# Linear attention beside an MLP: the tiles of y and of the MLP's activations begin 16 bytes later

## The chip, the core and the metric

The kernel runs on one core of one Trainium2 chip. The metric is the device time of one execution in microseconds, as the median of several runs. The kernel before takes 721.05 us (three runs, 720.82 to 721.19).

## The reference

A token matrix x of 2048 rows and 640 columns is normalised twice over. One branch is attention in linear form with 32 heads of 20; the other is an MLP of width 1728. The result is x plus both.

```python
xn = layernorm(x)
# A: linear attention with a learned feature map
q, k, v = split(xn @ wqkv)                       # 32 heads of 20
pq, pk = q @ w_phi, k @ w_phi                    # per head
phi = concat([softmax(p), softmax(-p)])          # for pq and pk
kv, z = phi_k^T v, sum(phi_k)
o = (phi_q kv) / (phi_q z + 1e-6)
# B: MLP
y = layernorm(xn)
h = gelu(y @ w1 + b1)
out = x + o @ wo + (h @ w2 + b2)
```

## The kernel before

Tokens are the columns of most tiles: the 2048 tokens are four blocks of 512, and the 640 features are five chunks of 128 partitions (`KC = 5`). All matrix products are in float32r, and each float32 operand is split exactly into a high and a low part (`split`, line 57), so that one product is three matmuls: high by high, high by low, low by high (`mm3`, lines 69 to 72). TensorE therefore runs some 3,300 matmuls, nearly all with a stationary operand of 128x128 and a streamed one of 512 columns.

The stages, in order:

- The first tokens are normalised and turned on TensorE into y of block 0 (`make_y0`), and y of block 1 is made from the transposed x (`next_y`, lines 413 to 445): POOL subtracts the mean (L438), DVE multiplies (L440), ACT rounds to the high part (L442), DVE subtracts for the low part (L444).
- MLP on blocks 0 and 1 (`Mlp.passes`): w1 is stationary and y is streamed (L70 to L72, `bank<-y,w`), ACT applies gelu (L264), the result is split into the m tiles, and w2 is stationary with the m tiles streamed (L70 to L72, `bank<-m,w`). DVE adds into acc (L307, L309). Beside it run small matmuls that fold w_phi into the projection weights (L499), and y of blocks 2 and 3 is made and put into DRAM (L589).
- The projections, one token tile of 128 after the other, 16 in all (`proj`, L673): y is stationary here, 128 columns of it, and the folded weights wkh, wkl (512, 512 and 320 columns) and v's weights (512 columns) are streamed. For each tile ACT, POOL and DVE make the two softmax features of k and q (`features`, L697 to L711, then L719, L764, L770), and `kv_tile` (L743, L747) accumulates phi_k and v. y of blocks 2 and 3 is loaded at tile 4 and tile 8 (L789), for use four tiles later.
- MLP on blocks 2 and 3, with the attention's products beside it (L967 and L968: kvs is stationary, and the feature tiles ph and e are streamed).
- The output projection (L1128 to L1136, again `mm3`): wo is stationary and the attention's result is streamed. It is split into tiles of the y pool (`Attention.split`, L1028 to L1032).

The order on TensorE is written by hand for the whole kernel (`manual_schedule`), and that of DVE, ACT and POOL for parts of it; `mlp.beside` is a generator from which one step is drawn after each group of matmuls.

The tiles come from pools that lie one behind another in each partition. From the bottom: the scratch for descriptors of DMAs that POOL would issue (16,384 bytes), constants, acc0 and acc1, the pool `m` (six tiles m0 to m5, from `mtile`, line 117: gelu's output, the split activations, and in the projections the features), the pool `y` (four tiles y00, y10, y01, y11), `raw` and `w`. A second side grows down from the top: x, the folded weights wkh and wkl, later acc2, acc3, kvs, ph and the e tiles. In the program as built, y00 begins at byte 68,064 of a partition, m4 at 38,368, w0 at 114,144, wkh at 175,584, kvs at 203,232. Each of these is 32 more than a multiple of 64, and so are the other tiles and slices of these names that matmuls read: every chunk, half and head group lies a multiple of 64 bytes from its tile's start. The exceptions are the tiles that L743 streams, whose slices step by 240 bytes, and small operands of the transposes and of L499 and L901 to L913.

Of the kernel before, what the change touches and what calls it, by code (L numbers as in the profile page):

```python
# [9 lines left out]
F32R = mybir.dt.float32r  # L10
# [5 lines left out]
P = 128  # L16
S, D, F, H, DH = 2048, 640, 1728, 32, 20
KC = D // P
# [23 lines left out]
SPREAD = [0] * 20 + [1] * 10 + [2] * 2  # L42
EPS = 1e-5
DEN_EPS = 1e-6


def f(ap):
    return ap.bitcast(F32)
# [3 lines left out]
def tile_kernel(ctx: ExitStack, tc: tile.TileContext, x, xT, wkT, wqT, wv, wphi, wo, w1, b1, w2, b2,  # L52
                ident, mmask, emask, vsel, out):
    nc = tc.nc
    ctx.enter_context(nc.allow_low_precision(reason="float32 operands are split exactly into float32r parts"))

    def split(hi, lo, src, scale=None, eng=nc.vector, first=nc.scalar):

        if scale is None:
            if first is nc.scalar:  # L60
                nc.scalar.activation(hi, src, AF.Copy)  # L61
            else:
                first.tensor_copy(hi, src)
            eng.tensor_tensor(lo, src, f(hi), op=ALU.subtract)  # L64
        else:
            nc.scalar.activation(hi, src, AF.Copy, scale=scale)
            nc.vector.scalar_tensor_tensor(lo, src, scale, f(hi), op0=ALU.mult, op1=ALU.subtract)
# [43 lines left out]
    mp = ctx.enter_context(tc.tile_pool(name="m", bufs=1))  # L111
    ys = ctx.enter_context(ExitStack())
    yp = ys.enter_context(tc.tile_pool(name="y", bufs=1))
    rp = ys.enter_context(tc.tile_pool(name="raw", bufs=1))
    wp = ys.enter_context(tc.tile_pool(name="w", bufs=1))

    def mtile(i, dtype=F32):
        return mp.tile([P, 2, D if i < 5 else 512], dtype, name=f"m{i}")
    y = {}

    def load_x(ts, xp, tag="xb"):
# [89 lines left out]
    class Mlp:  # L211
# [55 lines left out]
        def passes(self, g, b, ws, hid=None):  # L267
# [5 lines left out]
            if hid is None:  # L273
                hid, todo, gts = [], ws, mtile(4)
# [58 lines left out]
    dmas[1][0]()  # L333
    nc.scalar.dma_start(b1t, b1)
    nc.scalar.dma_start(b2t, b2)
    y[0], y[1] = ([yp.tile([P, KC, 512], F32R, name=f"y{p}{b}") for p in range(2)] for b in range(2))
    gts = mtile(4)
    hid = [mtile(2 * j + 1, F32R) for j in range(2)]
    hid = [(h[:, 0, :512], h[:, 1, :512]) for h in hid]
# [322 lines left out]
    def proj(t, i):  # L662

        yh, yl = y[t // 4]
        c = slice((t % 4) * P, (t % 4) * P + P)
        wh, wl = [w[:, :, slice(*CB[i])] for w in wkv_] if i < 3 else wv_
        ps = ptile()[:, :wh.shape[2]]
        ops = [(lh, rh, kc) for kc in range(KC) for lh, rh in ((yh, wh), (yh, wl), (yl, wh))]
        if i == 3:

            ops.sort(key=lambda op: op[1] is wh)
        for n, (lh, rh, kc) in enumerate(ops):
            nc.tensor.matmul(ps, lh[:, kc, c], rh[:, kc], start=n == 0, stop=n == 3 * KC - 1)  # L673
        return ps
# [11 lines left out]
    def evacuate(ps, n, f0):  # L686

        p3 = pks[n].rearrange("p (h f) -> p h f", f=DH)
        src = ps.rearrange("p (f h) -> p h f", h=H)
        return nc.scalar.activation(p3[:, :, 1 + f0:1 + f0 + src.shape[2]], src, AF.Copy).ins  # L690
# [23 lines left out]
    def k_tile(t):  # L714
        e, sm = features(t, "k")
        w = kp.tile([P, 2 * H], F32, name="w")
        nc.vector.reciprocal(w, sm)
        e3 = e.rearrange("p s (h f) -> p (s h) f", f=DH)
        nc.gpsimd.tensor_tensor(e3, e3, w.unsqueeze(2).to_broadcast([P, 2 * H, DH]), op=ALU.mult)  # L719
        ft = wp.tile([P, 4, D], F32R, name="w1")  # L720
        fh, fl = ft[:, 0:2], ft[:, 2:4]
        split(fh, fl, e)
        return ft

    def v_parts(t, ps, d0):

        v = vbuf[t % 2].rearrange("p (g c) -> p g c", c=VS)
        rs = rs_all[:, t:t + 1]
        n = DH - d0 if d0 else VF
        parts = []  # L730
        for g, m, w in ((0, 11, 3 * n),) if d0 else ((0, 10, 3 * n), (10, 1, 2 * n)):
            src = ps[:, 3 * g * n:3 * g * n + m * w].rearrange("p (g c) -> p g c", g=m)
            parts.append((src, *(v[:, g:g + m, c + 3 * d0:c + 3 * d0 + w] for c in (3, 67))))
        for src, hi, lo in parts:
            last = nc.scalar.activation(hi, src, AF.Copy, scale=rs)
        for src, hi, lo in parts:
            nc.vector.scalar_tensor_tensor(lo, src, rs, f(hi), op0=ALU.mult, op1=ALU.subtract)
        return last.ins
# [15 lines left out]
    def q_tile(t):  # L754


        e, sm = features(t, "q")
        w = kp.tile([P, 2 * H], F32, name="w")
        nc.vector.reciprocal(w, sm)
        e = e.rearrange("p s f -> p (s f)")  # L760
        for (hs, sv), (_, wv_), (_, ev) in zip(by_head(sm, 1), by_head(w, 1), by_head(e, DH)):
            nc.gpsimd.tensor_tensor(wv_[:, 1], sv[:, 0], wv_[:, 1], op=ALU.mult)
            shape = list(ev[:, 1].shape)
            nc.gpsimd.tensor_tensor(ev[:, 1], ev[:, 1], wv_[:, 1].to_broadcast(shape), op=ALU.mult)  # L764

        b, i = divmod(t, 4)
        if i == 0:
            ets[b] = [places[n % 5] for n in range(4 * b, 4 * b + 4)]
        for n, et in enumerate(ets[b]):
            nc.vector.transpose(et[:, :, 32 * i:32 * i + 32], e[:, 320 * n:320 * n + 320].rearrange("p (j r) -> p j r", r=32))  # L770

    def store_phi(b, n):

        ed = e_dram[b][320 * n:320 * n + 320, :].rearrange("(j r) (q n) -> q r j n", r=32, q=4)
        for q in range(4):
            nc.sync.dma_start(ed[q], ets[b][n][32 * q:32 * q + 32])
# [7 lines left out]
    for t, i in [(t, i) for t in range(14) for i in range(4)] + TAIL:  # L784
        if (t, i) in ((4, 0), (8, 0)):
            b = t // 4 + 1
            y[b] = [yp.tile([P, KC, 512], F32R, name=f"y{p}{b % 2}") for p in range(2)]
            for p in range(2):
                nc.sync.dma_start(f(y[b][p]), y_dram[b - 2][p])  # L789
        ps = proj(t, i)  # L790
        pq = 1 + t % 3
        if t and t % 4 == 0:
            store_phi(t // 4 - 1, i)
        if i == 0:
            evac = evacuate(ps, 0, 0)
        elif i == 1:
            evac = evacuate(ps[:, :KQ - 512], 0, 512 // H)
            fts[t] = k_tile(t)
            evacuate(ps[:, KQ - 512:], pq, 0)
        elif i == 2:  # L800
            evacuate(ps[:, C3 - C2:], pq, B1F)
            v_parts(t, ps, VF)
            q_tile(t)
        else:
            evac = v_parts(t, ps, 0)

        tk = {(15, 1): 13, (15, 3): 14}[t, i] if (t, i) in ((15, 1), (15, 3)) else t - 2 if 1 < t < 15 and i == 0 else None
        if tk is not None:
            kv_tile(tk, fts.pop(tk), vbuf[tk % 2])
        if i == 0 and t in (1, 2, 3, 6, 7):  # L810

            kc = (1, 2, 3, 6, 7).index(t)
            lo = rp.tile([P, D], F32, name="r1")
            hi = rp.tile([P, D], F32R, name="r2")
            nc.sync.dma_start(lo, wo[kc * P:(kc + 1) * P, :])
            with tc.issue_after(evac):
                split(hi, lo.bitcast(F32R), lo, eng=nc.gpsimd)
            for w, wd in zip((f(hi), lo), wo_dram):
                nc.sync.dma_start(wd[:, kc, :], w)
        if (t, i) == (11, 0):  # L820
            mlp = Mlp((0, 3, 2, 1), ((1, 2), (0, 3)))
            mlp.ph = ptile
            mlp.fetch(0)
        if (t, i) == (12, 3):
            with tc.issue_after(evac):
                ws = [mlp.take(0)]
            mlp.fetch(1)
        if (t, i) == (15, 3):
            w, late = mlp.take_parts(1)
            ws.append(w)  # L830
            late.pop(0)()
# [45 lines left out]
    def finish_kv(pxt):  # L877
# [9 lines left out]
        def done(tp, dens, mask, hi, lo):  # L887

            r, n, w = tp.shape
            nc.vector.tensor_scalar_add(dens, dens, DEN_EPS)  # L890
            km = sp.tile([G6, 5, VR], F32, name="km", bufs=2)[:r, :n, :w]
# [25 lines left out]
    class Attention:  # L917
# [99 lines left out]
        def split(self, c, eng):  # L1017

            b = self.b

            def tokens(ap):
                return ap.rearrange("p (q t n) -> p t q n", q=4, t=4)

            def parts(ap):
                return ap.rearrange("p (t q n) -> p t q n", q=4, t=4)

            if c == 0:
                self.oh, self.ol = (yp.tile([P, KC, 512], F32R, name=f"y{p}{b % 2}") for p in range(2))  # L1028
            if c < KC:
                nc.scalar.activation(parts(self.oh[:, c, :]), tokens(self.ob[:, c, :]), AF.Copy)  # L1030
            if c:
                eng.tensor_tensor(parts(self.ol[:, c - 1, :]), tokens(self.ob[:, c - 1, :]), f(parts(self.oh[:, c - 1, :])), op=ALU.subtract)  # L1032
            if c == KC and b < 2:

                acc[b] = op.tile([P, KC, 512], F32, name=f"ob{b}")
                nc.sync.dma_start(acc[b], a_dram[b])
# [163 lines left out]
```

## Time and profile before

| | |
|---|---|
| median of three runs | 721.05 us |
| profiled execution: its span | 719.3 us |
| TensorE busy | 710.7 us, 99% |
| weight loads | 598.2 us, 83% |
| DVE, ACT, POOL busy | 477.6, 323.0, 384.1 us |
| longest waits of TensorE | 2.3 us for DVE (L309), 1.3 us for POOL (L376), 1.0 us for ACT (L264) |

The span runs from the first to the last instruction of one profiled execution; the runs' time holds some 1.75 us more around it. PE is TensorE's matmuls and PEld its weight loads, which run under the matmul before. A matmul's row gives its start and a length that reaches into the next ones, because matmuls are pipelined: a 128x512 matmul is shown with some 0.39 us, and the next begins 0.23 us after it. What a matmul costs in a stream is therefore the distance from its start to the next start, and not its length.

### The profile page before, as it was taken

The numbers are of one execution on the slowest core, as the hardware profiler recorded it, in microseconds if no ns is written. First come the engines' busy times: TensorE is split into PE (matmuls) and PEld (weight loads), VectorE is DVE, ScalarE is ACT, GpSimd is POOL, SyncE is SP. The second block draws the span as 40 slices with busy tenths as digits, with TensorE's granted clock in tenths as the row PEclk, the third lists the DMA queues.
The fourth block names the chain that finished last, engine by engine and source line by source line (L and its number), as shares of the span: only waits on it lengthen the run. The fifth ranks groups of instructions, "written<-read, shape, count | busy, mean of one in ns | idle before, by whom it ended". The sixth has DMA issues, their size and how long they took to land.

```text
span 719.3 us, 9640 instructions
## 1 busy us (share of the span) xinstructions
PE 710.7 (99%) x3411; PEld 598.2 (83%) x3411; DVE 477.6 (66%) x787; ACT 323.0 (45%) x530; POOL 384.1 (53%) x332
## 2 busy tenths in 40 slices
PE   8989999999999999999999999999999999999998
PEld 7868888888888888888888887888888888888887
DVE  7776754757554788788898887635565566766432
ACT  6434454334334544545435446346565556530200
POOL 3521223345045997897878879346577787403000
PEclk9999999999999999999999999999999999999999
DMA  9803642656411227326302506943443443164122
GB/s 328 264 8 109 195 133 84 179 158 192 139 74 73 92 82 232 85 97 214 80 0 55 130 3 204 229 144 111 135 128 127 134 153 94 49 230 132 74 87 74
DMA packets 60454, 91.88 MB, mean 128 GB/s; under 512 B 7014, under 2 KB 31366, under 8 KB 59038
## 3 DMA queue, kind: packets, MB, share of 16 engines
q1 hardware_dynamic: 60102, 91.25, 40.7%
q8 instruction: 27, 0.44, 0.2%
q14 instruction: 21, 0.17, 0.1%
q10 hardware_dynamic: 304, 0.01, 0.0%
HBM read 63.51 MB, written 27.73 MB: 127 GB/s over the span
## 4 chain that ended last, share of the span: by engine, by line
PE 87%; DVE 3%; POOL 3%; ACT 1%; issue 1%; DMA 0%; SPq 0%; POOLq 0%
PE bank L673 23%; PE bank L70 18%; PE bank L72 18%; PE bank L71 18%; PE bank L743 2%; PE bank L499 2%; POOL m L708 2%; PE bank L967 1%; PE bank L968 1%; POOL m L719 1%; PE bank L305 1%; PE bank L285 1%; PE bank L304 1%; PE bank L286 1%; DVE sm L711 1%
## 5 line engine op out<-in xcount | busy, mean ns | idle before, releaser
L673 PE MATMUL bank<-wkh,y 128*128 128x512 f32 (+1 forms) x480 | 139.5, 364 | 0.0
L64 POOL TENSOR_TENSOR w<-r,w 128x640 fp32r<-128x640 f32 x52 | 83.3, 1619 | 95.6 <-ACT w L61 64.7
L70 PE MATMUL bank<-y,w 128*128 128x512 f32 (+1 forms) x334 | 129.8, 389 | 1.0 <-ACT m L264 1.0
L71 PE MATMUL bank<-y,w 128*128 128x512 f32 (+1 forms) x334 | 129.2, 387 | 0.0
L72 PE MATMUL bank<-y,w 128*128 128x512 f32 (+1 forms) x334 | 129.2, 387 | 0.0
L70 PE MATMUL bank<-m,w 128*128 128x512 f32 x260 | 102.4, 394 | 2.6 <-DVE acc L309 2.3
L72 PE MATMUL bank<-m,w 128*128 128x512 f32 x260 | 101.3, 389 | 0.0
L71 PE MATMUL bank<-m,w 128*128 128x512 f32 x260 | 101.2, 389 | 0.0
L673 PEld LDWEIGHTS bank<-wkh,y 128*128 128x128 f32 x480 | 87.5, 188 | 13.3
L309 DVE TENSOR_TENSOR acc<-bank,acc 128x512 f32<-128x512 f32 x120 | 81.1, 684 | 19.8 <-PE bank L72 11.8
L673 PE MATMUL bank<-wkl,y 128*128 128x512 f32 (+1 forms) x240 | 87.4, 364 | 0.0
L64 DVE TENSOR_TENSOR m<-m,m 128x512 fp32r<-128x512 f32 (+1 forms) x54 | 43.7, 814 | 65.5 <-ACT m L61 65.3
L70 PEld LDWEIGHTS bank<-y,w 128*128 128x128 f32 x334 | 62.7, 188 | 13.9 <-ACT m L264 1.2
L72 PEld LDWEIGHTS bank<-y,w 128*128 128x128 f32 x334 | 62.7, 188 | 12.8
L71 PEld LDWEIGHTS bank<-y,w 128*128 128x128 f32 x334 | 62.7, 188 | 12.5
L264 ACT ACTIVATE m<-bank,b1t 128x512 f32<-128x512 f32 (+1 forms) x54 | 36.2, 671 | 65.2 <-PE bank L72 61.0
L709 ACT ACTIVATE m<-m,rs_all 128x1280 f32<-128x1280 f32 x32 | 43.7, 1365 | 42.9 <-POOL m L708 42.9
L70 PEld LDWEIGHTS bank<-m,w 128*128 128x128 f32 x260 | 48.8, 188 | 14.4 <-DVE acc L309 3.5
L961 POOL TENSOR_TENSOR e<-e,m 128x512 fp32r<-128x512 f32 x28 | 36.2, 1295 | 41.8 <-ACT m L960 35.8
L711 DVE TENSOR_REDUCE sm<-m 128x64 f32<-128x1280 f32 x32 | 47.4, 1481 | 15.5 <-ACT m L709 15.4
L673 PE MATMUL bank<-w,y 128*128 128x512 f32 x240 | 57.4, 391 | 0.0
L72 PEld LDWEIGHTS bank<-m,w 128*128 128x128 f32 x260 | 48.8, 188 | 10.3
(156 smaller groups left out, 1249.3 us busy)
## 6 DMA issues: line engine op xcount, KB each, us to landing
r<-in_w SPq DMA_DIRECT2D x52, 320.0 KB
e<-e SPq DMA_DIRECT2D x40, 256.0 KB
e<-acc SPq DMA_DIRECT2D x52, 160.0 KB
acc<-in_xT SPq DMA_DIRECT2D x4, 1280.0 KB
xb<-in_x SPq DMA_DIRECT2D x8, 320.0 KB
t<-in_x SPq DMA_DIRECT2D x8, 320.0 KB
raw<-in_xT SPq DMA_DIRECT2D x10, 256.0 KB
yh<-t SPq DMA_DIRECT2D x10, 256.0 KB
```

What stands on the lines that cost most here:

```text
L64: eng.tensor_tensor(lo, src, f(hi), op=ALU.subtract)
L70: nc.tensor.matmul(ps, lh, rh, start=first, stop=False, **kw)
L71: nc.tensor.matmul(ps, lh, rl, start=False, stop=False, **kw)
L72: nc.tensor.matmul(ps, ll, rh, start=False, stop=last, **kw)
L264: nc.scalar.activation(gt, pz, AF.Gelu_apprx_tanh, bias=b1t[:, 2 * g + j:2 * g + j + 1])
L309: nc.vector.tensor_tensor(acc[b][:, m, :], pw, acc[b][:, m, :], op=ALU.add)
L499: nc.tensor.matmul(ps[:, u * nh * DF:(u + 1) * nh * DF], raw[:nh * DH, u * P:(u + 1) * P], wpt[:nh * DH, g, :nh, 1:], start=True, stop=True)
L673: nc.tensor.matmul(ps, lh[:, kc, c], rh[:, kc], start=n == 0, stop=n == 3 * KC - 1)
L708: subs[n, t] = nc.gpsimd.tensor_tensor(ep[:, s], a, b, op=ALU.subtract)
L709: exps[n, t] = nc.scalar.activation(e, e, AF.Exp, scale=rs_all[:, t:t + 1])
L711: nc.vector.tensor_reduce(sm, e.rearrange("p s (h f) -> p (s h) f", f=DH), axis=AX, op=ALU.add)
L961: nc.gpsimd.tensor_tensor(pl, e, f(ph), op=ALU.subtract)
```

## The change

Each tile of y and each m tile becomes 16 elements (64 bytes) longer, and what the kernel uses of it begins `SHIFT = 4` elements (16 bytes) after its start. The scratch for descriptors shrinks from 16,384 to 8,192 bytes, which makes the room. In the built program the tiles of the lower side come to lie 8,192 bytes further down, less 64 for each lengthened tile below them: w0 is at 106,592, which is again 32 more than a multiple of 64, while the used part of y00 begins at 60,272 and that of m4 at 30,192, both 48 more. What lies on the upper side (wkh, wkl, kvs, ph, e) stays where it was. All engines run the same instructions in the same order.

```diff
+SHIFT = 4
...
-    def mtile(i, dtype=F32):
-        return mp.tile([P, 2, D if i < 5 else 512], dtype, name=f"m{i}")
+    def shifted(pool, n, w, dtype, name):
+        return pool.tile([P, n * w + 16], dtype, name=name)[:, SHIFT:SHIFT + n * w].rearrange("p (n w) -> p n w", n=n)
+
+    def mtile(i, dtype=F32):
+        return shifted(mp, 2, D if i < 5 else 512, dtype, f"m{i}")
+
+    def ytile(p, b):
+        return shifted(yp, KC, 512, F32R, f"y{p}{b}")
...
-    y[0], y[1] = ([yp.tile([P, KC, 512], F32R, name=f"y{p}{b}") for p in range(2)] for b in range(2))
+    y[0], y[1] = ([ytile(p, b) for p in range(2)] for b in range(2))
...
-            y[b] = [yp.tile([P, KC, 512], F32R, name=f"y{p}{b % 2}") for p in range(2)]
+            y[b] = [ytile(p, b % 2) for p in range(2)]
...
-                self.oh, self.ol = (yp.tile([P, KC, 512], F32R, name=f"y{p}{b % 2}") for p in range(2))
+                self.oh, self.ol = (ytile(p, b % 2) for p in range(2))
...
-    nc = bacc.Bacc("TRN2", target_bir_lowering=False, num_devices=1)
+    nc = bacc.Bacc("TRN2", target_bir_lowering=False, num_devices=1, dynamic_dma_scratch_size=8192)
```

## The prediction

> **What bounds the kernel now.** I read the page's sums first, then the busy time by stretches, then the order in time on TensorE, then the chain of waits.
>
> ```profile
> span 719.3 us, 9640 instructions
> PE 710.7 (99%) x3411; PEld 598.2 (83%) x3411; DVE 477.6 (66%) x787; ACT 323.0 (45%) x530; POOL 384.1 (53%) x332
> PE 87%; DVE 3%; POOL 3%; ACT 1%; issue 1%; DMA 0%; SPq 0%; POOLq 0%
> ```
>
> TensorE works for 99% of the span and carries 87% of the chain that ended last. So the question is what one matmul costs, not what TensorE waits for. By stretches:
>
> ```profile
> 0.00:42.36 42.36, 38.09 (x184) 30.64 (x184) 33.45 (x81) 22.29 (x39) 21.11 (x18) 1.00 0.73 251
> 42.36:225.00 182.64, 182.48 (x863) 152.63 (x864) 109.40 (x193) 73.14 (x127) 55.15 (x40) 1.00 0.42 132
> 225.00:393.50 168.50, 168.50 (x865) 145.57 (x865) 140.35 (x207) 85.41 (x131) 138.85 (x142) 1.00 0.33 97
> 393.50:443.40 49.90, 48.91 (x259) 42.31 (x258) 39.93 (x54) 26.46 (x40) 43.12 (x40) 1.00 0.42 121
> 443.40:719.30 275.90, 272.69 (x1245) 227.01 (x1245) 154.49 (x254) 115.71 (x195) 125.82 (x95) 1.00 0.40 126
> ...
> 480.00:700.00 220.00, 220.00 (x972) 182.19 (x971) 128.42 (x209) 99.83 (x167) 105.75 (x79) 1.00 0.38 122
> ```
>
> Columns: stretch, length, then busy time and count of PE, PEld, DVE, ACT, POOL, then the granted clock, the DMA share and GB/s. The clock is 1.00 throughout, so no throttle is in play. From 480 to 700 us TensorE is never idle, all its matmuls there are 128x512, and 220.00 / 972 is 226.3 ns a matmul; single rows further down give 0.226 to 0.227 us, and I use 226.7. For the 256-column matmuls near the end:
>
> ```profile
> 714.13 0.28 PE L70 MATMUL bank<-y,w 128*128 128x256 f32 x1
> ...
> 715.69 0.28 PE L71 MATMUL bank<-y,r 128*128 128x256 f32 x1
> ```
>
> Thirteen steps lie between these starts, 1.56 / 13 = 120 ns each. The 256 further columns of a full matmul therefore cost 226.7 - 120 = 106.7 ns, or 0.417 ns a column; 512 columns are 213.3 ns, and **13.3 ns of every matmul, wide or narrow, are a toll beside the columns**. Every matmul has one weight load of 128 columns under it, and this is what does not change with the width. 13.3 ns are 32 columns' time, and a weight row of 128 fp32 is 32 lines of 16 bytes. The Trainium skill (SBUF — State Buffer, Specifications) gives 16 bytes as the line of this memory; no row here shows a line.
>
> **Is the toll a collision of two reads?** For it speaks what happens after TensorE has been disturbed:
>
> ```profile
> 434.41 0.40 PE L71 MATMUL bank<-y,w 128*128 128x512 f32 x1
> 434.65 0.39 PE L72 MATMUL bank<-y,w 128*128 128x512 f32 x1
> ...
> 435.35 0.39 PE L72 MATMUL bank<-y,w 128*128 128x512 f32 x1
> 435.57 0.39 PE L70 MATMUL bank<-y,w 128*128 128x512 f32 x1
> ...
> 436.73 0.39 PE L72 MATMUL bank<-y,w 128*128 128x512 f32 x1
> ...
> 437.86 0.39 PE L71 MATMUL bank<-y,w 128*128 128x512 f32 x1
> ```
>
> The ten steps from 434.41 to 436.73 average 232 ns, and singles differ (240 ns at the first, 220 ns from 435.35, in these rounded starts); then five settled steps take 1.13 / 5 = 226 ns. Nothing is waited for there. A fixed handover would cost the same each time; a toll that depends on how the stream of the running matmul and the load of the next one's weights stand to each other in time would swing like this and settle. Against it speaks a matmul with no load under it:
>
> ```profile
> 35.99 0.39 PE L71 MATMUL bank<-m,w 128*128 128x512 f32 x1
> 36.22 0.39 PE L72 MATMUL bank<-m,w 128*128 128x512 f32 x1
> 36.75 0.50 PE L70 MATMUL bank<-m,w 128*128 128x512 f32 x1
> ```
>
> The one at 36.22 has nothing behind it until 36.75 and is shown as long (0.39) as its neighbours. The page says that ends of matmuls are modelled, so I give this row less weight than the starts, but it keeps the rival of a fixed toll alive.
>
> **The change part by part.** No instruction is added, removed or moved on any engine; each keeps its shape. What changes is where tiles begin.
>
> *The stream against the weights.* Before, the streamed operand and the weights both begin 32 bytes past a multiple of 64, in every matmul that counts. After, y and the m tiles begin 48 past, and w, wk, kvs and the v tiles still 32, so each stream of y or m is 16 bytes away from the weight row loaded under it, as is each wk stream from the y loaded under it. How many:
>
> ```profile
> L70 PE MATMUL bank<-y,w 128*128 128x512 f32 x326 | 127.6, 391 | 1.0 <-ACT m L264 1.0
> L673 PE MATMUL bank<-wkh,y 128*128 128x512 f32 x320 | 104.0, 392 | 0.0
> L70 PE MATMUL bank<-m,w 128*128 128x512 f32 x260 | 102.4, 394 | 2.6 <-DVE acc L309 2.3
> L673 PE MATMUL bank<-wkl,y 128*128 128x512 f32 x160 | 62.7, 392 | 0.0
> L673 PE MATMUL bank<-w,y 128*128 128x512 f32 x240 | 57.4, 391 | 0.0
> L673 PE MATMUL bank<-wkh,y 128*128 128x320 f32 x160 | 37.8, 309 | 0.0
> L673 PE MATMUL bank<-wkl,y 128*128 128x320 f32 x80 | 24.7, 309 | 0.0
> L968 PE MATMUL bank<-e,kvs 128*128 128x512 f32 x44 | 17.1, 389 | 0.0
> ```
>
> L673 has 960; L70 has 586, and L71 and L72 as many each, 1,758; smaller forms (L348, L285, L286, L304, L305, L967 from m, the 256-wide ones, those on r) add 255: 2,973 matmuls change. L968 reads e, which is not shifted, and is my control.
>
> *Which of them are on the path.* Two stretches are set by other engines:
>
> ```profile
> 32.98 1.25 POOL xb L438
> ...
> 42.36 0.50 PE bank L70
> ...
> 382.85 10.64 PE bank L673 x52
> ...
> 437.07 2.89 POOL m L708 x3
> ...
> 443.40 0.50 PE bank L70
> ```
>
> These are pieces of the chain of waits. From 32.98 to 42.36 it runs through POOL, DVE and ACT, which make y of block 1, and from 393.49 (382.85 + 10.64) to 443.40 through the features of the last tokens, 50 us without TensorE. Faster matmuls in the first 42 us and in those 50 us become waiting. So the 144 changed matmuls of the first stretch (184 less the 18 of the warm-up and 22 transposes) and some 226 of the fourth (259 less three tiles of 11 at L743 and L747) don't count: 2,973 - 370 = about 2,600 do. In 225 to 393 us DVE (140.35 of 168.50) and POOL (138.85) are 82 to 83% busy; 744 matmuls shorter by 11 ns (168.5 to 160.3 us) bring them to 87 or 88%, which I take as still covered. If that cover failed, the 744 changed matmuls of that stretch would drop out and 8 us of the gain with them.
>
> *What each gains.* No row has a stream and a load standing 16 bytes apart for a whole matmul, so this is bounded, not read. One end is the whole toll, 13.3 ns gained. The other is a loss: the settled phase is the cheapest that lasts, and others averaged 232 ns, 5.4 ns more. I take 11 ns gained, near the first end: a toll of one step per line of the weight row looks like two streams in step, and putting them a line apart should take out nearly all of it, with some 2 ns left for the handover itself. 2,600 x 11 ns = 28.6 us. The Trainium skill (TensorE: Matmul & The Clock Gate, Back-to-back issue gap) has N/2.4 + 2.5 ns for a warm matmul, 215.8 ns for 512 columns, where the trace has 226.7; by it 10.9 ns could go, and the sum would be 28.3 us.
>
> *The rest, at nothing.* Elementwise work on shifted tiles keeps its shapes and its 64-byte steps:
>
> ```profile
> L264 ACT ACTIVATE m<-bank,b1t 128x512 f32<-128x512 f32 x50 | 34.4, 688 | 64.8 <-PE bank L72 60.6 <-DVE m L64 2.5 <-DVE ra L158 0.9
> ```
>
> ACT stands idle 64.8 us before these for want of work; a few per cent on 688 ns is hidden. DMAs now write y 16 bytes off:
>
> ```profile
> y<-yh SPq DMA_DIRECT2D x2, 1280.0 KB
> ...
> 258.11 1.12 PE bank L743 x10
> ...
> 271.83 1.12 PE bank L743 x10
> ```
>
> The chain's rows at 258.11 and 271.83 show one token tile, 13.7 us; y is fetched four tiles ahead, about 55 us for 2.56 MB. At the 97 GB/s moved in that stretch it takes 27 us, and twice that still fits; without the cover the excess would stall L673. The halved scratch serves DMAs issued from POOL, and the trace has none there: nothing.
>
> *Sum.* The profiled execution is 719.3 us; the median run 721.05 has 1.75 us around it. 719.3 - 28.6 + 1.75 = **692.4 us**, 4.0% faster.
>
> **The rivals.** *A, part of the toll goes.* If the two streams drift through each other and only half is saved, 2,600 x 6.65 = 17.3 us: 703.7. The swinging steps after a restart speak for a drift.
>
> *B, a fixed toll.* The 13.3 ns are the price of changing weights in this format, whatever the addresses; the change then does not do what it could: 721. For it: the lone matmul at 36.22, and that all widths pay alike. Against it: the swing from 220 to 240 ns with nothing else changed. The Trainium skill (TensorE: Matmul & The Clock Gate, Step-by-step: what each phase is for) says that the array has two independent read ports and that loading the next weights takes nothing from the running matmul; by that rule B holds and the time is 721. Its own 2.5 ns leave the trace's 13.3 unexplained.
>
> *C, slower.* The present equal start is the lucky one: it locks into 226.7, while after disturbances the steps average 232. Shifted by a line, the streams lock into, or wander among, such dearer phases; 5.4 ns x 2,600 is 14.0 us, and 1.2 us more from the 226 matmuls in 393 to 443 us, where TensorE is busy 48.91 of 49.90 us and so soon sets the end itself: 736. It decides as soon as the settled step is above 227.3 ns (0.55 ns x 2,600 is 1.4 us, 0.2%). At the worst step of the restart, 0.24 us, the toll doubles: 13.3 ns x 2,826 = 37.6 us, 759.
>
> **How the numbers follow.** Nearly all of it goes (forecast): 0.47. A: 0.12. B: 0.13. C: 0.28. A change under 0.2% (1.4 us) can't be told from none. Faster is the forecast and A, 0.59; same is B, 0.13; slower is C, 0.28. The forecast's own range is 685 (13.3 ns on 2,600 matmuls: 686.5, and a little more from the covered stretches) to 699. The stated range must hold A, B and half of C, so it reaches from 685 to 737; beyond it lie the dearer half of C and a little below.
>
> **What would show it.** Right: matmul starts at L70 to L72 about 216 ns apart in a stretch without waiting, L673 likewise, but 226 to 227 at L968, whose stream is not shifted; PE's wait at 393 to 443 us grown by 2 to 3 us; DVE and POOL nearer 88% in the middle. A shows steps between 217 and 225. B shows 226.7 unchanged, C steps of 230 or more, or steps that never settle. The forecast is wrong if the settled step is above 224, or if DVE or POOL sets the pace of the middle and the 13.7 us per token tile stay.

## The result, and the profile after

The changed kernel takes 733.28 us (median of 4 runs, 733.20 to 733.42); the kernel before took 721.03 us beside it (4 runs). The ratio is 1.0171 [1.0156, 1.0185]: 12.25 us slower, where 28.6 us of gain were forecast. The profiled execution has a span of 731.5 us, 12.2 us more than before.

The sums of the page of the kernel after, with the shares of the chain that ended last by engine:

```profile
span 731.5 us, 9639 instructions
PE 723.0 (99%) x3411; PEld 598.1 (82%) x3411; DVE 477.0 (65%) x787; ACT 323.8 (44%) x530; POOL 384.4 (53%) x332
PE 87%; POOL 3%; DVE 3%; ACT 1%; issue 1%; DMA 0%; POOLq 0%
```

TensorE is busy 12.3 us longer with the same 3,411 matmuls; DVE, ACT, POOL and the weight loads are where they were, within 1 us. The shape of the chain is the same too. So nothing new is waited for: the matmuls themselves are dearer. Busy time by stretches of the kernel after, columns as in the prediction:

```profile
42.36:225.00 182.64, 182.50 (x844) 149.75 (x844) 107.68 (x191) 72.31 (x125) 54.72 (x39) 1.00 0.43 132
225.00:393.50 168.50, 168.50 (x858) 144.01 (x857) 136.30 (x199) 84.30 (x128) 135.18 (x137) 1.00 0.31 94
...
480.00:700.00 220.00, 220.00 (x950) 178.14 (x949) 128.14 (x209) 102.35 (x171) 110.99 (x83) 1.00 0.39 121
```

In the stretch from 480 to 700 us TensorE is never idle, as before, and the granted clock is 1.00, as before. But 950 matmuls fit where 972 did: 231.6 ns each instead of 226.3. Single matmuls show that this is no settled state. First some rows of the order in time on TensorE of the kernel before, then of the kernel after (start, shown length):

```profile
599.68 0.39 PE L71 MATMUL bank<-m,w 128*128 128x512 f32 x1
599.91 0.39 PE L72 MATMUL bank<-m,w 128*128 128x512 f32 x1
...
602.63 0.39 PE L70 MATMUL bank<-y,w 128*128 128x512 f32 x1
602.86 0.39 PE L71 MATMUL bank<-y,w 128*128 128x512 f32 x1
```

```profile
599.84 0.39 PE L71 MATMUL bank<-y,w 128*128 128x512 f32 x1
600.06 0.40 PE L72 MATMUL bank<-y,w 128*128 128x512 f32 x1
600.30 0.40 PE L73 MATMUL bank<-y,w 128*128 128x512 f32 x1
...
601.69 0.40 PE L73 MATMUL bank<-y,w 128*128 128x512 f32 x1
601.93 0.40 PE L975 MATMUL bank<-ph,kvs 128*128 128x512 f32 x1
602.16 0.39 PE L976 MATMUL bank<-e,kvs 128*128 128x512 f32 x1
602.39 0.39 PE L71 MATMUL bank<-y,w 128*128 128x512 f32 x1
```

(After the change, L70 to L72 are L71 to L73, and the lines of the projections and behind them lie 8 further down.) Before, 14 steps from 599.68 to 602.86 take 3.18 us, 227 ns each. After, the 11 from 599.84 to 602.39 take 2.55 us, 232 ns, and singles go from 220 to 240 ns in the middle of a run without waiting, as they did before only behind a disturbance. L975 from ph and L976 from e, whose operands begin where they did before, take 0.23 us each, like the others.

Where the 12.2 us fall, by the chain of waits, first of before, then of after:

```profile
216.13 28.25 PE bank L673 x135
...
245.58 12.53 PE bank L673 x60
```

```profile
42.26 0.50 PE bank L71
...
219.10 28.89 PE bank L681 x135
...
249.18 12.74 PE bank L681 x60
...
388.44 10.64 PE bank L681 x52
...
443.04 2.88 POOL m L716 x3
...
449.36 0.50 PE bank L71
```

| part of the chain | before, us | after, us | more |
|---|---|---|---|
| to the first L70 / L71 | 42.36 | 42.26 | -0.1 |
| to the end of the last x52 of the projections | 351.13 | 356.82 | 5.7 |
| the last tokens' features, through POOL, DVE, ACT | 49.91 | 50.28 | 0.4 |
| to the end | 275.90 | 282.14 | 6.2 |

From the starts in the two traces: the second part has 1,298 matmuls of 512 columns and they went from 227.75 to 232.46 ns (4.71 ns x 1,298 = 6.1 us); the last has 1,163, from 226.72 to 232.18 ns (5.46 x 1,163 = 6.4 us). Matmuls of 320, 256 and 240 columns stayed within some 1.2 ns of what they were. The two parts make 12.5 us, which accounts for the time. (All "steps" below are counted this way: distances between neighbouring starts, in the trace, of matmuls of 512 columns, those over 260 ns left out as waits.)

### The profile page after: what moved, and what is told of

It is laid out like the page before. It is cut to its first block, busy times and chain, and to the rows that moved or that the text cites. A ratio compares the mean times of both kernels' runs of the same rounds, so it can differ in the third digit from the quotient of the medians.

```text
span 731.5 us, 9639 instructions
## 1 busy us (share of the span) xinstructions
PE 723.0 (99%) x3411; PEld 598.1 (82%) x3411; DVE 477.0 (65%) x787; ACT 323.8 (44%) x530; POOL 384.4 (53%) x332
## 4 chain that ended last, share of the span: by engine, by line
PE 87%; POOL 3%; DVE 3%; ACT 1%; issue 1%; DMA 0%; POOLq 0%
PE bank L681 23%; PE bank L71 18%; PE bank L72 18%; PE bank L73 18%; PE bank L751 2%; PE bank L507 2%; POOL m L716 2%; PE bank L976 1%; PE bank L975 1%; POOL m L727 1%; PE bank L294 1%; PE bank L313 1%; PE bank L293 1%; PE bank L312 1%; PE bank L909 1%
## 5 line engine op out<-in xcount | busy, mean ns | idle before, releaser
L681 PE MATMUL bank<-wkh,y 128*128 128x512 f32 (+1 forms) x480 | 141.5, 368 | 0.0
L71 PE MATMUL bank<-y,w 128*128 128x512 f32 (+1 forms) x334 | 131.2, 393 | 0.5 <-ACT m L272 0.5
L72 PE MATMUL bank<-y,w 128*128 128x512 f32 (+1 forms) x334 | 131.2, 393 | 0.0
L73 PE MATMUL bank<-y,w 128*128 128x512 f32 (+1 forms) x334 | 130.6, 391 | 0.0
L71 PE MATMUL bank<-m,w 128*128 128x512 f32 x260 | 103.4, 398 | 2.4 <-DVE acc L317 2.3
L72 PE MATMUL bank<-m,w 128*128 128x512 f32 x260 | 102.6, 395 | 0.0
L73 PE MATMUL bank<-m,w 128*128 128x512 f32 x260 | 102.4, 394 | 0.0
L71 PEld LDWEIGHTS bank<-y,w 128*128 128x128 f32 x334 | 62.8, 188 | 15.5 <-ACT m L272 0.7
L73 PEld LDWEIGHTS bank<-y,w 128*128 128x128 f32 x334 | 62.7, 188 | 14.2
L72 PEld LDWEIGHTS bank<-y,w 128*128 128x128 f32 x334 | 62.8, 188 | 13.9
L71 PEld LDWEIGHTS bank<-m,w 128*128 128x128 f32 x260 | 48.9, 188 | 15.1 <-DVE acc L317 3.2
L73 PEld LDWEIGHTS bank<-m,w 128*128 128x128 f32 x260 | 48.9, 188 | 11.3
L72 PEld LDWEIGHTS bank<-m,w 128*128 128x128 f32 x260 | 48.9, 188 | 10.8
```

Of the source, the lines that this page charges most:

```text
L71: nc.tensor.matmul(ps, lh, rh, start=first, stop=False, **kw)
L72: nc.tensor.matmul(ps, lh, rl, start=False, stop=False, **kw)
L73: nc.tensor.matmul(ps, ll, rh, start=False, stop=last, **kw)
```

## What could cause it

The addresses of the built programs change the question. Before, the tiles in question are whole multiples of 256 bytes long, and the starts given above for y00, m4, w0, wkh and kvs all leave 224 when divided by 256. So nearly every stream begins a multiple of 256 bytes from the weight row loaded under it (over 2,600 of 2,668). After, each y and m tile is longer by 64 bytes, and what lies above it moves by 64 more. From y00 at 60,272 to w0 at 106,592 are 46,320 bytes, 181 x 256 - 16: four lengthened tiles lie in between, which make a whole 256, and the shift alone remains. From m4 at 30,192 to w0 are 76,400, 299 x 256 - 144: with ten lengthened tiles, 128 bytes come on top of the 16. The change thus does two things, a shift of 16 bytes and a spread of distances over multiples of 64. The theories for the runs: the shift itself (the distance between stream and weight row, modulo 32 or 64; or the stream's own start); the re-laid memory (longer tiles, smaller scratch); and, from the second step on, the distance modulo 256 (S).

## Experiments

**1. Only the lengthening.**

```diff
-SHIFT = 4
+SHIFT = 0
```

> The longer tiles and the halved scratch, but nothing begins later (SHIFT = 0): all streams and weight rows 32 past a multiple of 64 as before. Theory D (the distance between the start of the stream and that of the weight row decides whether the two settle into 226.7 ns steps): 721 us, steps of 226.7. Theory O (a stream or a row that begins 16 bytes past a multiple of 32 costs more by itself): 721 too. Theory R (the moved bases or the scratch do it): 733, steps about 232.5.

731.45 us (731.36 to 731.57), ratio 1.0145 [1.0130, 1.0160]. The stretch from 480 to 700 us of this kernel:

```profile
480.00:700.00 220.00, 220.00 (x950) 177.87 (x949) 127.97 (x209) 102.29 (x171) 109.54 (x81) 1.00 0.39 121
```

950 matmuls, as after the full change, though every start is again 32 past a multiple of 64. The steps average 231.7 ns. By distance modulo 256 they are 231.7 at 0 (826 steps), 231.5 at 64 (503), 231.7 at 128 (629) and 231.8 at 192 (714): a matmul at distance 0 among neighbours at other distances costs as much as they do. The shift, and modulo 32 or 64, are out as the sole cause; 10.5 of the 12.25 us come without any shift.

**2. Everything shifted alike.** y, m, the weights, kvs, v, e and ph all begin 16 bytes later.

```diff
-            w = wp.tile([P, 4, D], F32R, name=f"w{self.slots[c % 4]}")
+            w = shifted(wp, 4, D, F32R, f"w{self.slots[c % 4]}")
...
-    kvs = bp.tile([P, 11, P], F32R, name="kvs")
+    kvs = shifted(bp, 11, P, F32R, "kvs")
```

> y, m and also every weight tile, kvs, v, e and ph begin 16 bytes later, so stream and weight row are level again, both 48 past a multiple of 64. D: 721 us, settled steps of 226.7. O: 733 or more, steps of 232 or more, since nothing begins on a multiple of 32.

730.31 us, ratio 1.0133 [1.0116, 1.0150]; steps of 231.3 ns. Equal starts modulo 64 don't bring the time back. The distances modulo 256 are spread over multiples of 64 here too, since the same tiles and more are 64 bytes longer.

**3. A shift of 32 bytes.**

```diff
-SHIFT = 4
+SHIFT = 8
```

> y and m begin 32 bytes later instead of 16, weights as before: stream and row are 32 apart modulo 64, and both begin on multiples of 32. O: 721 us, 226.7. D with a period of 32 bytes: 721 and 226.7; D with a period of 64: not 721, about 733 if the steps don't settle, and less than 721 if 32 apart is a better distance.

734.46 us, ratio 1.0187 [1.0172, 1.0202]; steps of 232.8 ns. With every start on a multiple of 32 the loss is at least as large, so it isn't a matter of 16 bytes.

**4. Streams with one distance each.** A kernel of its own: 40 matmuls of 512 columns in a row at one distance, then seven of 240 columns as a disturbance, then the next 40. Nothing else runs beside it; runs 4, 8 and 9 are one execution each, with a granted clock of 1.00 in the streams. Starts are counted from those of the two tiles.

```diff
+            a, c = sw + 128 * (k % 8), sm + 512 * (k % 4)
+            nc.tensor.matmul(ps[:wcols, :cols], w[:, a:a + wcols], s[:, c:c + cols], start=True, stop=True)
```

> No part of the reference is computed: only streams of 40 matmuls, with the start of the stream (sm) and of the weight row (sw) changed from job to job, each after seven short matmuls that disturb TensorE. D: steps depend on sm - sw alone; 226.7 at 0, about 232 at 4 elements (16 bytes), and sm = sw = 4 gives 226.7 again. O: sm = sw = 4 gives 232 or more, and 8 and 16 elements give 226.7. If the toll is a collision of reads, narrower weights (96, 64, 32 columns) pay less, in proportion (10, 6.7, 3.3 ns of the 13.3), and if it is a fixed price of a change of weights, they pay 13.3 all the same. Some distance may give less than 226.7; 215 would mean that the toll can be avoided.

The mean of the last 20 steps, by the distance in bytes, with the weights 128 columns wide:

| 0 | 16 | 32 | 48 | 64 | 80 | 96 | 112 | 128 | 192 | 256 | 512 |
|---|---|---|---|---|---|---|---|---|---|---|---|
| 226.7 | 231.7 | 233.3 | 233.3 | 229.0 | 230.9 | 233.2 | 230.8 | 233.3 | 233.3 | 226.7 | 226.7 |

Rows of the order in time: a stream at distance 0, one at 16, and one whose weights instead of the stream begin 16 bytes later, a distance of -16:

```profile
28.14 9.25 PE L91 MATMUL bank<-s,w 128*128 128x512 f32 x40
37.22 0.94 PE L87 MATMUL bank<-s,w 128*128 128x240 f32 x7
38.00 9.43 PE L91 MATMUL bank<-s,w 128*128 128x512 f32 x40
47.27 0.94 PE L87 MATMUL bank<-s,w 128*128 128x240 f32 x7
...
188.92 9.49 PE L91 MATMUL bank<-s,w 128*128 128x512 f32 x40
198.25 0.95 PE L87 MATMUL bank<-s,w 128*128 128x240 f32 x7
```

From the first start to the disturbance behind the stream are 9.08, 9.27 and 9.33 us, 227.0, 231.8 and 233.2 ns a matmul with the unsettled ones at the beginning. Of the distances in the table only 0, 256 and 512 settle; the others go on in a pattern of dear and cheap steps. No address gave less than 226.7 for 512 columns. Narrower weights at distance 0 are dearer, not cheaper: 230.0, 229.7 and 231.7 ns for 96, 64 and 32 columns. The toll beside the columns is 13.3 ns for streams of 384 and 256 columns as well, and 16.7 for 480. At 256 columns, though, 120.0 is only the mean of steps from 117 to 124 ns, and a distance of 16 bytes gives 118.7 there, a toll of 12.0.

**5. The lengthening as 256 bytes, no shift**, with the smaller scratch and all bases moved.

```diff
-SHIFT = 4
+SHIFT, PAD = 0, 64
...
-        return pool.tile([P, n * w + 16], dtype, name=name)[:, SHIFT:SHIFT + n * w].rearrange("p (n w) -> p n w", n=n)
+        return pool.tile([P, n * w + PAD], dtype, name=name)[:, SHIFT:SHIFT + n * w].rearrange("p (n w) -> p n w", n=n)
```

> Tiles longer by 64 elements (256 bytes) instead of 16, nothing begins later, scratch halved. Theory S (the steps settle into 226.7 only where stream and weight row begin a multiple of 256 bytes apart; the 64 bytes by which each tile was lengthened spread the distances over 0, 64, 128 and 192): all distances are 0 modulo 256 again, 721 us, 226.7 ns. Theory R (the halved scratch, or that tiles moved at all): 731 as with 64 bytes.

721.02 us (10 runs), ratio 1.0000 [0.9991, 1.0009].

```profile
480.00:700.00 220.00, 220.00 (x972) 182.19 (x971) 128.51 (x209) 100.04 (x167) 105.97 (x79) 1.00 0.39 123
```

972 matmuls again. Longer tiles, the halved scratch and other bases cost nothing; it was the 64 bytes, as distances modulo 256.

**6 and 7. The shift alone**, 16 and 64 bytes, on tiles that are 256 bytes longer (`SHIFT, PAD = 4, 64` and `SHIFT, PAD = 16, 64`).

> As e5, and y and m begin 16 bytes later: the shift alone, without the spread of distances. S, priced by the streams of e4 (231.7 ns at 16 bytes): 5 ns x about 2,830 matmuls = 14 us, 735. If only the spread mattered: 721. If the shift alone gains what was forecast: 692.

> As e5, and y and m begin 64 bytes later: distances 64 (some 1,880 matmuls) and, where y is the weight, 192 (945). S, priced by e4 (229.0 at 64 bytes, 233.3 at 192): 2.3 ns x 1,880 + 6.6 ns x 945 = 10.6 us, 731.5; and TensorE's steps at L70 to L72 (distance 64) nearer to 229 than in e6. If only the bits below 64 bytes mattered: 721.

728.65 us, ratio 1.0106 [1.0089, 1.0122], and 728.36 us, 1.0102 [1.0086, 1.0117]: both dearer, but less than expected. Run 6 first, then run 7:

```profile
480.00:700.00 220.00, 220.00 (x951) 178.58 (x950) 127.40 (x208) 100.87 (x169) 108.32 (x81) 1.00 0.39 122
```

```profile
480.00:700.00 220.00, 220.00 (x959) 179.92 (x959) 128.27 (x210) 102.52 (x171) 109.87 (x81) 1.00 0.39 122
```

The late MLP, where y and m are streamed, has 951 in run 6, as after the full change. By distance the steps of run 6 are 231.7 ns at 16 bytes (1,884 steps) and 227.6 at 240 (692: here the shifted y is the weight and wk the stream, so the distance is -16). The expectation had put 5 ns on all of them. In run 7 they are 229.3 ns at 64 (1,882) and 233.3 at 192 (695), which the streams of run 4 priced at 229.0 and 233.3; there the expectation counted too many matmuls on the path.

So the lengthening alone makes 10.5 us, the shift alone 7.6, both together 12.25 rather than 18: a step that doesn't settle anyway gets hardly worse by a second reason.

**8. The period.** Streams as in run 4, every 32 bytes up to 512, both starts moved alike, and other formats.

> No part of the reference is computed: streams of 40 matmuls as in e4. S: distances of 32 to 512 bytes in steps of 32 give 226.7 only at 256 and 512 and 229 to 234 between; stream and row shifted alike by 32, 48, 64, 80 or 128 bytes give 226.7 if the distance alone counts, and more at those that aren't a multiple of 32 if the start counts too (at 16 bytes e4 had 231.1). If the toll is a fixed price of a matmul, weights of 16 and 2 columns still pay 13 ns or more; if it comes from the load's reads they pay next to nothing. Streams that alternate between two distances: 226.7 for 0 and 256, unsettled for 0 and 64, 0 and 128, 0 and 16. Operands of bf16 (half the bytes) pay 2 to 3 ns by the Trainium skill (TensorE: Matmul & The Clock Gate, Back-to-back issue gap): 216; if the toll is one of the array and not of the memory, 226.7 as well.

Some rows of the order in time, for distances of 32, 224 and 256 bytes, 2-column weights, and bf16 operands at distance 0 and 16 bytes (8 elements):

```profile
27.85 9.48 PE L97 MATMUL bank<-s,w 128*128 128x512 f32 x40
37.17 0.95 PE L90 MATMUL bank<-s,w 128*128 128x240 f32 x7
...
88.40 9.49 PE L97 MATMUL bank<-s,w 128*128 128x512 f32 x40
97.73 0.95 PE L90 MATMUL bank<-s,w 128*128 128x240 f32 x7
98.52 9.25 PE L97 MATMUL bank<-s,w 128*128 128x512 f32 x40
107.61 0.94 PE L90 MATMUL bank<-s,w 128*128 128x240 f32 x7
...
298.67 9.43 PE L97 MATMUL bank<-s,w 128*2 128x512 f32 x40
307.94 0.95 PE L90 MATMUL bank<-s,w 128*128 128x240 f32 x7
...
318.63 8.81 PE L97 MATMUL bank<-sb,wb 128*128 128x512 bf16 x40
327.09 1.14 PE L90 MATMUL bank<-s,w 128*128 128x240 f32 x7
328.07 8.81 PE L97 MATMUL bank<-sb,wb 128*128 128x512 bf16 x40
336.52 1.14 PE L90 MATMUL bank<-s,w 128*128 128x240 f32 x7
```

To the start behind them, 40 matmuls take 9.32, 9.33 and 9.09 us, 9.27 with two columns of weights, and 8.46 and 8.45 in bf16. In the settled half: 233.3, 228.8, 233.4, 233.3, 234.2, 233.3, 233.3 and 226.7 ns for 32, 64, ... 256 bytes, and the same eight values again from 288 to 512: the period is 256 bytes. Starts moved alike give 226.7 for 32, 64 and 128 bytes, but 230.0 to 231.1 for 16, 48 and 80: the distance isn't all, the start itself counts too. Streams that alternate between 0 and 256 bytes settle at 226.7; between 0 and 64, 128 or 16 they take 231.7, 230.0 and 232.5. Weights of 16 columns take 231.7 ns, like those of 2. bf16 takes 215.8 ns, a toll of 2.5 ns, at each of the three distances tried (0, 16 and 128 bytes); the 8.46 us above are shorter than 40 such steps because the disturbance starts 28 ns after the last bf16 matmul.

**9. Narrow weights, single strays, and 240 bytes.**

> No part of the reference is computed: streams of matmuls as in e4 and e8. Two jobs walk: stream and weight row both begin 0, 64, 128, 192 bytes later in turn. In walk 1 a matmul's stream is level with its own weights and 64 off the weights loaded while it runs; in walk 2 it is level with the weights loaded while it runs, that is the next matmul's. If the distance that counts is that to the load running under the stream: walk 2 settles at 226.7 and walk 1 doesn't; if it is that to its own weights, the reverse. Weights of 2 and of 64 columns at distances of 0 to 256 bytes: if the toll were a collision with the load's own reads, 2 columns would make all distances alike, near 216; after e4 and e8 I expect 228 to 234 at all of them. One stray matmul, 64 bytes off, in every 40, 20 or 10: if the settled state is lost by one stray and found again after about ten, the mean rises from 226.7 by about 1, 2 and 4 ns; if a stray costs only itself, by 0.1 to 0.6. Widths from 416 to 504 columns: a settled toll of 13.3 ns at those where the step is a multiple of 13.3 ns, more at the others.

Two-column weights take 231.4 to 231.7 ns at 0, 32, 64, 128, 192 and 256 bytes (235.4 at 16), and 64-column weights 228.3 to 232.7, at none of these distances 226.7. One matmul off by 64 bytes among matmuls at distance 0 has a step of 237 ns, and behind it come 241, 224, 231, 236, 228, 233, 230 and then 227 ns: some 47 ns lost on eight steps. With one stray in ten the mean is 231.2 ns, in twenty 228.8, in forty 227.8, as expected if the settled state is lost by one stray. Of the further widths, 416 columns have the toll of 13.3 ns; 448, 496 and 504 have 16.0 to 16.7, so that 504 columns take as long as 512. The row with one in ten, and the stream at 240 bytes:

```profile
292.31 27.90 PE L101 MATMUL bank<-s,w 128*128 128x512 f32 x120
320.05 0.96 PE L90 MATMUL bank<-s,w 128*128 128x240 f32 x7
...
341.12 9.23 PE L101 MATMUL bank<-s,w 128*128 128x512 f32 x40
```

27.74 us for 120 are 231.2 ns each. At 240 bytes the stream settles at 226.7, like 0 (9.23 us shown for 40, against 9.25 at 256 bytes in run 8), which is what run 6 had at the projections. But the distance of -16 that run 4 made by moving the weights took 233.3, so that the distance alone doesn't decide here. Two series in which the start of the stream walks by 64 bytes from matmul to matmul, level either with its own weights or with those loaded under it, settled in neither case (230.3 and 231.7 ns); which of the two pairs counts stays open.

## Why the prediction was wrong

*What bounds the kernel: right.* The steps on TensorE set the time; other engines' busy time and the waits stayed, and the time went where full-width matmuls on the path are.

*"13.3 ns of every matmul ... are a toll beside the columns": right as a number at 512, 384 and 256 columns, wrong as something to be gained.* Settled streams of 512 columns have it at every address where they settle, and none was below it. It isn't the same for every width (16.0 to 16.7 ns at 448 to 504 columns, and 12.0 at 256 columns with a distance of 16 bytes).

*The step that failed: "a toll of one step per line of the weight row looks like two streams in step, and putting them a line apart should take out nearly all of it".* The term was 11 ns gained a matmul; measured are 5.0 ns lost (227.36 to 232.34 over all), and with the shift alone, in run 6, 3.2 ns (230.6). The match of 13.3 ns with 32 lines of a weight row was a match of two numbers. If the toll were one step per line of the weight row it would shrink with the row; it is 18.4 ns with a row of two columns (run 8). What the runs put in its place: for 512 columns 13.3 ns is the floor, reached in a settled state, and dearer states lie above it. The swing after a disturbance, which I took for a sign that the toll could be removed, showed how the dearer state looks. The Trainium skill (TensorE: Matmul & The Clock Gate, Back-to-back issue gap) has N/2.4 + 2.5 ns for a warm matmul, from which 215.8 ns for 512 columns is an estimate; the bf16 streams of run 8 have just that, and the float32r streams never did, so that figure was no bound for this kernel.

*"Both begin 32 bytes past a multiple of 64" was the wrong unit.* The traces could not show it, but the starts in the built program could: before, they agree modulo 256, and 64 bytes more per tile break that. Run 1 shows that this side of the edit, which I costed at nothing because "64-byte steps" were kept, makes 10.5 us by itself, more than the shift's 7.6. Of the other things costed at nothing (the scratch, moved bases, elementwise work on the shifted tiles) run 5 confirms the first two, and the unchanged busy times of DVE, ACT and POOL the third.

*The control failed.* L968 was to stay at 226 to 227 ns, its stream not being shifted; its steps are 231 ns after the change. It was no clean control there, for the weights loaded under its stream are those of w, which moved by 128 bytes modulo 256. But it takes 231 ns in runs 6 and 7 too, where its stream and both weight rows begin as before, modulo 256. Run 9 shows why: the state is carried from one matmul to the next, and one stray spoils its own step and the seven behind it.

*Rival C came true* in its sign, with its idea that "the present equal start is the lucky one", and nearly in its size, 736 us. The size is in part luck: C put it all down to the shift, and the shift alone (run 6) costs 7.6 us, about half of what C had. Its terms: 5.4 ns more per step, measured 5.0 (227.36 to 232.34 over all); 2,600 matmuls, where it should have been the 2,461 of full width in the two parts that TensorE sets, since narrower ones didn't change; and 1.2 us for the last tokens' features, measured 0.4. The lengthening, which costs more than the shift, isn't in it.

*Rival B* has the fixed toll right and the indifference to addresses wrong. The Trainium skill (TensorE: Matmul & The Clock Gate, Step-by-step: what each phase is for) has loading take nothing from the running matmul. The two-column weights agree, since a smaller load made no matmul cheaper; but with 128 columns the distance between stream and weight row moves the step from 226.7 to 234.2 ns (run 8), which independent reads alone would not do. With two columns the distances of 0 to 256 bytes in run 9 differ by 0.3 ns only. That fits a distance that acts through the load's reads; no run shows how.

*Open:* what the toll is physically, which pair of starts counts, and why -16 settles like 0 when the stream is 240 bytes on (run 9) and at the projections of run 6, but not when the weights of a stream are moved by 16 (run 4). No version tried was faster than the kernel before; run 5 equals it.

## What to carry to other kernels

Where float32r matmuls of 512 columns and 128-column weights stand end to end, keep every streamed operand a multiple of 256 bytes from the weight row loaded under it, and both on multiples of 32: pad tiles by whole 256 bytes, and look at the addresses of the built program whenever a tile's length changes. A fixed excess per instruction isn't a collision because its size fits one: vary the supposed cause (here the width of the weights) in a small kernel before costing its removal. And an equal start that looks accidental may be what a settled state stands on, so that the scatter of steps behind a disturbance shows what there is to lose, not to gain.

## What the runs showed of the hardware

- float32r, 512 columns, 128-column weights: 226.7 ns settled; at other distances, 240 aside, 228 to 235 ns with starts on multiples of 16 bytes (up to 236.7 with a start one element off, run 4), mostly in patterns that repeat, and none of them at 226.7 within 40 matmuls.
- The period of the distance is 256 bytes, in steps of 32. A distance of +16 doesn't settle; one of -16 did in one of two streams (run 9, not run 4) and in run 6.
- The state has a memory: one stray 64 bytes off costs some 47 ns on eight steps, and one in ten raises the mean to 231.2 ns, more than a stream that is off by 64 bytes throughout (229.0).
- The toll does not grow with the weights: 13.3 ns for 128 columns, 18.4 for two, at distance 0. With 2 to 96 columns no stream settled at 226.7.
- bf16 operands show no such dependence: 215.8 ns at the three distances tried.
